# A decode step with its gradients: which small sums share a PSUM bank

## The chip, the cores and the metric

The kernel runs on one core of a Trainium2 chip. The metric is the device time of one execution in microseconds (us). Three runs of the kernel before gave 719.51, 720.91 and 721.76 us, a median of 720.91 us. A separate profiled execution took 720.1 us, of which 718.3 us are the span that the profile covers.

## The reference

One token of width 640 goes through attention over a cache of 8192 keys and values (32 heads of width 128) and, beside it, through a gated layer. The kernel returns the output and the gradients with respect to the token, the caches and the five weight matrices.

```python
def _A_ref(x, k_cache, v_cache, wq, wo):                       # 32 heads, Dh = 128, Sk = 8192
    q = (x @ wq).reshape(B, Sq, Hq, Dh).transpose(0, 2, 1, 3)
    scores = jnp.einsum("bhqd,bhkd->bhqk", q, k) * (Dh ** -0.5)
    p = _softmax(scores, axis=-1)
    o = jnp.einsum("bhqk,bhkd->bhqd", p, v)
    return o.transpose(0, 2, 1, 3).reshape(B, Sq, Hq * Dh) @ wo

def _B_ref(x, w1, w3, w2):                                     # D = 640, F = 1728
    return (_silu(x @ w1) * (x @ w3)) @ w2

xn = _layernorm(x)
out = x + _A_ref(xn, k_cache, v_cache, wq, wo) + _B_ref(xn, w1, w3, w2)
# returned: out, and the gradients of x, k_cache, v_cache, wq, wo, w1, w3, w2 for grad_out
```

For each head the gradients of the two caches are outer products: dV is the probabilities P times the vector do, dK is the score gradients U times the query q. Each is as large as the cache itself, 2 MB a head, so a head reads 4 MB and writes 4 MB.

## The kernel before

A head's 8192 positions lie on 128 partitions with 64 positions (J) each. K and V of a head are tiles of 128 x 64 x 128 in bf16. The kernel first does the gated layer, whose weights are small, and then loops over the heads. The order on every engine is the order of the program text, written out by hand (`manual_schedule`), and the loop is staggered: iteration h finishes head `c` = h, starts head `n` = h + 1 and keeps head `prev` = h − 1's last copy.

One iteration of the loop (lines 717 to 769) runs in this order. The names in capitals of the profile are: PE the TensorE, DVE the VectorE, ACT the ScalarE, POOL the GpSimd engine, SP the queue engine.

- `product(n, "S", 0)`: DVE multiplies half of K by the query into T (L403), PE adds T up with eight matmuls into `psS` (L405).
- `probs(c)`: DVE reads the sum of the exponentials and inverts it (`rZ`, L463), DVE and ACT make P and Pf.
- `outer` (V, half 0): DVE (L425) and ACT (L419, eight instructions) write the outer product into `ot`.
- `keep_dq(prev)`, then a `gap()`, in which one step of a group's preparation or finish may run on ACT and PE.
- `row_dots(c)`: DVE reduces `psDP`, and PE sums the products over the partitions (L503).
- `attend(c)`: sixteen matmuls of V with P into `ob` (L474), and once in a group `on_sums` (L341); `turn_wq(c)`: transposes on PE.
- `product(n, "S", 1)`, `outer` (V, half 1) and its store on POOL's queue (L432), the load of the next V on SP's queue.
- `dscores(c)`: DVE makes U from the sum of L503 (L507), PE adds sixteen matmuls of K with U into `ob`.
- `outer` (K, half 0); ACT copies `ob` out (`wide`, L482) and the turned wq (L522).
- `row_max(n)`: DVE reduces `psS` and takes the row maximum, PE spreads the maxima over the partitions (L450).
- `product(n, "DP", 0)`, and then `blocks_sum(c)`: PE picks o and dq out of `wide` with four f32 matmuls (L490; the profile shows each f32 matmul as two).
- `outer` (K, half 1) and its store, the load of K three heads on, a `gap()`.
- `exps(n)`: DVE reads the spread maxima (`negM`, L455), ACT exponentiates (L458), PE sums over the partitions (L459).
- `product(n, "DP", 1)`.
- `weights(c)`: DVE reads o and dq (`odq`, L527), ACT makes `dq_diag` and `om` from it, PE broadcasts dq (L533), collects o in columns for the group (L538) and adds dq through the turned wq to dxn (L541).

PSUM, the memory that PE writes to, has eight banks of 512 f32 columns on 128 partitions. `accbank` is one bank: columns 0 to 4 hold the running sum dxn (L541), 5 to 9 the running sum out (L341 and L658), 16 to 23 the columns `on_ps` of two groups (written by L538, read by ACT in `on_cols`, L332), 32 to 35 `od` of two heads (written by L490, read by L527). `sm` is another bank, taken anew for each head at L449: column 3 the softmax sum (L459), column 4 the dot sum (L503), columns 8 to 135 the spread maxima (L450). `psS` and `psDP` share two banks, `ob` has one, and three banks (`ps_w`) serve the rest, among them `dx_ps`, in which the dx of the gated layer is summed in parts (`dx_part`).

A matmul's `start` flag says that it opens a sum, `start=False` that it adds to one. dxn and out are never opened by a flag: the bank's first 16 columns are set to zero at L222.

Queues: loads of K and V go out on SP's queue, most stores on POOL's queue. In the profile a store's issue on POOL shows the instruction that the store waited for. `turn_lanes` issues a small load into `lane_pad` on POOL's queue: the kernel counts in `dealt` which of 16 lanes the next transfer of that queue begins at, and the load's number of rows moves that lane on. At iteration H − 3 the stores collected in `late` are issued on POOL, followed by one `turn_lanes(0)`; the stores of the last two heads go out on SP, so nothing follows on POOL.

Of the kernel before, what the change touches and what calls it, by code (L numbers as in the profile page):

```python
# [10 lines left out]
F32 = mybir.dt.float32  # L11
# [5 lines left out]
P = 128  # L17
# [4 lines left out]
def kernel(  # L22
# [80 lines left out]
    with tc.manual_schedule(engines=ORDERED):  # L103
# [29 lines left out]
        def turn_lanes(to):  # L133
            k = (to - dealt[0]) % LANES
            if k:
                rows = k if k > 1 else LANES + 1
                nc.gpsimd.dma_start(lane_pad[0:rows, dealt[1] % 2], wq_v[0:rows, 0:2, 0:8])
                dealt[:] = to % LANES, dealt[1] + 1

        def deal(dst, src, p0, p1):  # L140
            nc.gpsimd.dma_start(dst[p0:p1], src[p0:p1])
            dealt[0] = (dealt[0] + (LANES - 1 if p0 == 0 else P - p0)) % LANES
# [79 lines left out]
        nc.vector.memset(accbank[:, 0:16], 0.0)  # L222
        DXN0 = 0
        OUT0 = NC
        OP0 = 16
        OD0 = 32

        sel = consts.tile([P, P // GH], F32, name="sel")
        nc.vector.tensor_reduce(sel[:], ident_f[:].rearrange("p (q r) -> p q r", r=GH), AX.X, ALU.add)
# [214 lines left out]
        def row_max(st):  # L444
            st.S = small.tile([P, J], F32, name="S_sb", bufs=1)
            nc.vector.tensor_reduce(st.S[:], st.ps["S"][:], AX.X, ALU.add)  # L446
            mrow = small.tile([P, 1], F32, name="mrow")
            nc.vector.tensor_reduce(mrow[:], st.S[:], AX.X, ALU.max)  # L448
            st.sm = ps_s.tile([P, 512], F32, name="sm", tag="sm")  # L449
            nc.tensor.matmul(st.sm[:, 8:8 + P], lhsT=mrow[:].to_broadcast([P, P]), rhs=ident_f[:], start=True, stop=True,  # L450
                             skip_group_check=True)

        def exps(st):
            negM = small.tile([P, 1], F32, name="negM")
            nc.vector.tensor_reduce(negM[:], st.sm[:, 8:8 + P], AX.X, ALU.max, negate=True)  # L455
            st.E = small.tile([P, J], F32, name="E", bufs=1)
            rsum = small.tile([P, 1], F32, name="rsum")
            nc.scalar.activation(st.E[:], st.S[:], ACTF.Exp, bias=negM[:], scale=1.0, accum_out=rsum[:])  # L458
            nc.tensor.matmul(st.sm[:, 3:4], lhsT=ones_f, rhs=rsum[:], start=True, stop=True, skip_group_check=True)  # L459

        def probs(st):
            rZ = small.tile([P, 1], F32, name="rZ")
            nc.vector.reciprocal(rZ[:], st.sm[:, 3:4])  # L463
            st.P2 = small.tile([P, J, 2], BF16, name="P2")
            nc.vector.tensor_scalar(st.P2[:], st.E[:].unsqueeze(2).to_broadcast([P, J, 2]), rZ[:], None, ALU.mult)
            st.Pf = small.tile([P, 2, ACT_J], F32, name="Pf")
            nc.scalar.activation(st.Pf[:], st.E[:].rearrange("p (a j) -> p a j", a=2)[:, :, JH - ACT_J:JH],  # L467
                                 ACTF.Copy, scale=rZ[:])
# [15 lines left out]

        def blocks_sum(st):
            c0 = OD0 + 2 * (st.h % 2)
            st.od = accbank[:, c0:c0 + 2]
            for r in range(WIDE):
                i, b = divmod(r, WIDE // 2)
                nc.tensor.matmul(st.od, lhsT=st.wide[i][:, b * DH:(b + 1) * DH], rhs=pick[:, r, :],  # L490
                                 start=(r == 0), stop=(r == WIDE - 1), skip_group_check=True)
# [6 lines left out]
        def row_dots(st):  # L498
            st.DP = small.tile([P, J], F32, name="DP_sb", bufs=1)
            nc.vector.tensor_reduce(st.DP[:], st.ps["DP"][:], AX.X, ALU.add)  # L500
            rdot = small.tile([P, 1], F32, name="rdot")
            nc.vector.scalar_tensor_tensor(st.S[:], st.DP[:], 1.0, st.P2[:, :, 0], ALU.mult, ALU.mult, accum_out=rdot[:])
            nc.tensor.matmul(st.sm[:, 4:5], lhsT=ones_f, rhs=rdot[:], start=True, stop=True, skip_group_check=True)  # L503

        def dscores(st):
            st.U2 = small.tile([P, J, 2], BF16, name="U2", bufs=1)
            nc.vector.scalar_tensor_tensor(st.U2[:], st.DP[:].unsqueeze(2).to_broadcast([P, J, 2]), st.sm[:, 4:5], st.P2[:],  # L507
                                           ALU.subtract, ALU.mult)
            st.Uf = None
            if st.h < H - 1:  # L510
                st.Uf = small.tile([P, 2, ACT_J], F32, name="Uf")
                nc.vector.tensor_copy(st.Uf[:], st.U2[:, :, 0].rearrange("p (a j) -> p a j", a=2)[:, :, JH - ACT_J:JH])  # L512
            wide_sums(st.K, st.U2, 1)
# [10 lines left out]
        def weights(st):  # L524
            G_, hh = st.G, st.hh
            odq = small.tile([P, 2], F32, name="odq")
            nc.vector.tensor_tensor(odq[:], st.od, sc2[:], ALU.mult)  # L527
            odq_bf = small.tile([P, 1], BF16, name="odq_bf")
            nc.vector.tensor_copy(odq_bf[:], odq[:, 1:2])
            dq_diag = small.tile([P, P], BF16, name="dq_diag", bufs=1)  # L530
            nc.scalar.activation(dq_diag[:], ident_bf[:], ACTF.Copy, scale=odq[:, 1:2])  # L531
            st.ps_db = ps_w.tile([P, DH], F32, name="ps_db", tag="w")
            nc.tensor.matmul(st.ps_db[:], lhsT=ones_bf[:], rhs=dq_diag[:], start=True, stop=True)  # L533
            om = small.tile([P, GH], F32, name="om")
            nc.scalar.activation(om[:], rmask[:], ACTF.Copy, scale=odq[:, 0:1])
            if hh == 0:
                G_["on_ps"] = accbank[:, OP0 + GH * (st.g % 2):OP0 + GH * (st.g % 2 + 1)]
            nc.tensor.matmul(G_["on_ps"][hh * (P // GH):(hh + 1) * (P // GH), :], lhsT=sel[:], rhs=om[:],  # L538
                             start=True, stop=True, skip_group_check=True)
            for ci in range(NC):  # L540
                nc.tensor.matmul(accbank[:, DXN0 + ci:DXN0 + ci + 1], lhsT=st.wqT[:, ci * P:(ci + 1) * P],  # L541
                                 rhs=odq_bf[:], start=False, stop=True, skip_group_check=True)
# [59 lines left out]
        def dx_part(wi, wt, c0, n):  # L602
            T = tpool.tile([P, n, F], BF16, name="T13", tag="T")
            nc.vector.tensor_tensor(T[:], wt[:, c0:c0 + n, :],
                                    bc_sb[:, wi, :].unsqueeze(1).to_broadcast([P, n, F]), ALU.mult)
            for i in range(F // DR1):
                nc.tensor.matmul(dx_ps[:, c0:c0 + n, :], lhsT=ident_bf[:], rhs=T[:, :, DR1 * i:DR1 * (i + 1)],  # L607
                                 start=(wi == 1 and i == 0), stop=(wi == 0 and i == F // DR1 - 1),
                                 skip_group_check=True)

        def grad(wi, wt):
# [82 lines left out]
        def gap():  # L694
            if steps and next(steps[0], "end") == "end":
                steps.pop(0)

        ob = ps_o.tile([P, 512], F32, name="ob", tag="ob")
        nc.tensor.matmul(ob[:], lhsT=ident_bf[:], rhs=zero_bf[:].to_broadcast([P, WIDE * DH]), start=True, stop=True)
        first = new_head(0)  # L700
# [16 lines left out]
        for h in range(H - 1):  # L717
            n = new_head(h + 1) if h + 1 < H else None
            c = hs.pop(h)
            g, hh = divmod(h, GH)  # L720
            if n:
                product(n, "S", 0)
            probs(c)
            outer(c, c.do, c.P2, c.Pf, "V", h, 0)
            if prev:
                keep_dq(prev)
            gap()
            row_dots(c)
            attend(c)
            turn_wq(c)  # L730
            if n:
                product(n, "S", 1)
            outer(c, c.do, c.P2, c.Pf, "V", h, 1)
            if h + 2 < H:
                load_v(h + 2)
            wq_columns(h, 0)
            gap()
            dscores(c)
            outer(c, c.q, c.U2, c.Uf, "K", h, 0)
            keep_rows(c)  # L740
            keep_wq(c)
            if hh == 1 and 0 < g < NG - 1:
                load_wo(g + 1, nc.scalar)
            wq_columns(h, 1)
            if n:
                row_max(n)
                product(n, "DP", 0)
            blocks_sum(c)
            outer(c, c.q, c.U2, c.Uf, "K", h, 1)
            if h == 0:  # L750
                load_k(4)
            elif 1 < h < H - 3:
                load_k(h + 3)
            wq_columns(h, 2)
            if h == H - 3:
                for by, dst, src in late:
                    by(dst, src)
                turn_lanes(0)
            gap()
            if n:  # L760
                exps(n)
                product(n, "DP", 1)
            weights(c)
            gap()
            if hh == 1 and g + 1 < NG:
                steps.append(prep_steps(g + 1))
            if hh == 2:
                gap()
            prev = c
# [88 lines left out]
```

## Time and profile before

| | us |
|---|---|
| median of three runs | 720.91 (719.51 to 721.76) |
| the profiled execution | 720.1 |
| its span | 718.3 |
| DVE busy | 630.6 |
| PE busy (matmuls) | 552.2 |
| ACT busy | 479.3 |
| POOL busy | 49.5 |

The profile gives the time at which each engine was busy with instructions, the granted TensorE clock (1.00 is full speed) and the busy share of the core's 16 DMA engines, all for the whole span or for a chosen stretch. A line of the timeline reads: start in us, duration in us, engine, line of the kernel, operation, what is written from what, with the partitions and elements, and how many instructions were merged; in brackets stands how long the engine was idle before, and what ended the idle time. A line of the waits reads: engine, tile and line that waited, the one waited for, and then us in total, number of times and the longest. The chain of work that ended last gives these shares of the span:

```
DMA 41%; DVE 28%; PE 22%; ACT 5%; issue 1%
```

### The profile page before, as it was taken

To read this page: it belongs to the slowest core of one execution; us is meant where nothing else is said; L and a number is where in the kernel's file an instruction comes from. 1 tells how busy PE (TensorE), PEld (TensorE's weight loads), DVE (VectorE), ACT (ScalarE), POOL (GpSimd) and SP (SyncE) were. 2 spreads that over 40 slices of the span, in tenths; PEclk is the share of its full clock that TensorE was granted. 3 is DMA by queue.
4 is the path that set the end of the run, shared out by engine and by line. 5 is a ranking of instruction groups with operands and counts; after the bars stand their busy time and mean duration, and the time that the engine had idled before them with its cause. 6 is when DMAs were issued, how large, how long until landed. Compare 5 with 4: busy or idle time off the path is not lost.

```text
span 718.3 us, 10242 instructions
## 1 busy us (share of the span) xinstructions
PE 552.2 (77%) x3698; PEld 277.9 (39%) x3698; DVE 630.6 (88%) x722; ACT 479.3 (67%) x1455; POOL 49.5 (7%) x91
## 2 busy tenths in 40 slices
PE   5787788778888797787788787488887878777770
PEld 3653344334444343343343344143443334333330
DVE  5789999899999996798899899499998989999982
ACT  2166666796678856596577866468667957777552
POOL 0010000000000210000000110000000000000100
PEclk9699998997998988799899889889989899999995
DMA  8999999999999999999999999999999999999997
GB/s 354 414 428 425 430 429 430 390 428 428 432 430 429 429 425 426 428 427 429 432 431 428 430 427 424 429 428 427 431 432 428 429 430 430 428 430 431 429 423 309
DMA packets 27696, 303.35 MB, mean 422 GB/s; under 512 B 3264, under 2 KB 3974, under 8 KB 9982
## 3 DMA queue, kind: packets, MB, share of 16 engines
q1 hardware_dynamic: 13490, 154.89, 51.0%
q0 software_dynamic: 10960, 137.72, 45.1%
q10 hardware_dynamic: 3196, 10.10, 3.5%
q8 instruction: 29, 0.48, 0.2%
q14 instruction: 21, 0.17, 0.1%
HBM read 151.34 MB, written 151.34 MB: 421 GB/s over the span
## 4 chain that ended last, share of the span: by engine, by line
DMA 41%; DVE 28%; PE 22%; ACT 5%; issue 1%; SPq 0%; POOL 0%; DVEq 0%; ACTq 0%; POOLq 0%
DMA Kt<-in_A_k_cache_dram 24%; DVE T L403 14%; DMA out_dram<-ot 10%; DVE ot L425 8%; PE ob L474 5%; PE psS L405 5%; PE psDP L405 5%; DMA lane_pad<-in_A_wq_dram 4%; ACT ot L419 3%; DMA Vt<-in_A_v_cache_dram 3%; DMA dbc<-in_B_w_dram 2%; PE accbank L490 1%; DVE DP_sb L500 1%; DVE S_sb L446 1%; PE dx_ps L607 1%
## 5 line engine op out<-in xcount | busy, mean ns | idle before, releaser
L405 PE MATMUL psDP<-T,ident_bf 128*128 128x512 bf16 x512 | 152.2, 451 | 62.1 <-DVE T L403 61.9
L405 PEld LDWEIGHTS <-ident_bf 128*128 128x128 bf16 x1024 | 108.3, 109 | 199.9 <-issue 125.6
L419 ACT ACTIVATE ot<-qs_g,Uf 128x128 bf16<-128x128 bf16 x496 | 151.7, 393 | 41.9 <-DVE Uf L512 26.8
L403 DVE TENSOR_TENSOR T<-Kt,qs_g 128x4096 bf16<-128x4096 bf16 x64 | 146.3, 2286 | 17.4 <-DMA Kt<-in_A_k_cache_dram 16.9
L419 ACT ACTIVATE ot<-do_g,Pf 128x128 bf16<-128x128 bf16 x504 | 153.9, 389 | 1.1
L403 DVE TENSOR_TENSOR T<-Vt,do_g 128x4096 bf16<-128x4096 bf16 x64 | 146.0, 2282 | 2.9 <-ACT do_g L323 1.6
L405 PE MATMUL psS<-T,ident_bf 128*128 128x512 bf16 x512 | 130.2, 400 | 14.9 <-DVE T L403 14.0
L425 DVE TENSOR_TENSOR ot<-qs_g,U 128x3072 bf16<-128x3072 bf16 (+1 forms) x64 | 113.1, 1768 | 13.3 <-DMA out_dram<-ot 13.3
L425 DVE TENSOR_TENSOR ot<-do_g,P 128x3072 bf16<-128x3072 bf16 (+1 forms) x64 | 112.8, 1762 | 6.8 <-DMA out_dram<-ot 5.8
L432 POOL DMA_DIRECT2D out_dram<-ot x60 | 32.2, 537 | 549.9 <-DVE Uf L512 279.3
L474 PE MATMUL ob<-Kt,U 128*4 128x512 bf16 x512 | 60.5, 379 | 1.3 <-DVE U L507 1.3
L474 PE MATMUL ob<-Vt,P 128*4 128x512 bf16 x512 | 61.0, 381 | 0.0
L531 ACT ACTIVATE dq_diag<-ident_bf,odq 128x128 bf16<-128x128 bf16 x32 | 12.8, 401 | 47.2 <-DVE odq L527 47.2
L490 PEld LDWEIGHTS accbank<-pick,wide 128*128 128x128 f32 x256 | 40.1, 223 | 7.8 <-issue 2.4
L467 ACT ACTIVATE Pf<-E,rZ 128x16 f32<-128x16 f32 x32 | 9.8, 305 | 48.4 <-DVE rZ L463 48.4
L297 ACT COPY woT<-ps_t 128x512 bf16<-128x512 bf16 x40 | 23.0, 576 | 21.5 <-PE ps_t L292 21.5
L490 PE MATMUL accbank<-pick,wide 128*128 128x2 f32 x256 | 35.6, 261 | 0.5 <-ACT wide L482 0.5
L450 PE MATMUL sm<-ident_f,mrow 128*128 128x128 f32 x64 | 16.0, 334 | 23.5 <-DVE mrow L448 23.5
L474 PEld LDWEIGHTS <-U 128*4 128x4 bf16 x512 | 19.8, 84 | 36.7 <-DVE U L507 5.2
L474 PEld LDWEIGHTS <-P 128*4 128x4 bf16 x512 | 19.9, 84 | 25.4 <-issue 0.8
L446 DVE TENSOR_REDUCE S_sb<-psS 128x64 f32<-128x512 f32 x32 | 21.9, 685 | 6.0 <-PE psS L405 6.0
L482 ACT COPY wide<-ob 128x256 f32<-128x256 f32 x64 | 19.9, 360 | 8.9 <-PE ob L474 8.9
(165 smaller groups left out, 538.3 us busy)
## 6 DMA issues: line engine op xcount, KB each, us to landing
out_dram<-ot POOLq DMA_DIRECT2D x60, 2048.0 KB, 24.8
Kt<-in_A_k_cache_dram SPq DMA_DIRECT2D x32, 2048.0 KB, 26.4
Vt<-in_A_v_cache_dram SPq DMA_DIRECT2D x32, 2048.0 KB, 21.1
out_dram<-ot SPq DMA_DIRECT2D x8, 1024.0 KB, 13.3
out_dram<-wo_g ACTq DMA_DIRECT2D x6, 640.0 KB, 15.9
wo_g<-in_A_wo_dram ACTq DMA_DIRECT2D x6, 640.0 KB, 15.4
wq<-in_A_wq_dram SPq DMA_DIRECT2D x2, 1280.0 KB, 33.7
w1t<-in_B_w_dram SPq DMA_DIRECT2D x1, 2160.0 KB, 12.3
```

The source lines that it names most:

```text
L297: nc.scalar.copy(woT[:], ps_t[:])
L403: nc.vector.tensor_tensor(T[:], src[:, :, ds_], vec[:, ds_].unsqueeze(1).to_broadcast([P, J, DHH]), ALU.mult)
L405: nc.tensor.matmul(ps[:], lhsT=ident_bf[:], rhs=T[:, :, RUN * i:RUN * (i + 1)], start=(half == 0 and i == 0), stop=(half == 1 and i == DHH ...
L419: nc.scalar.activation(st.ot[half][:, JH - ACT_J + j].rearrange("p a b -> p (a b)"), vec, ACTF.Copy, scale=wf[:, half, j:j + 1])
L425: nc.vector.tensor_tensor(st.ot[half][:, 0:n], vec.rearrange("p (a b) -> p a b", b=2).unsqueeze(1).to_broadcast([P, n, DH // 2, 2]), w2[:, ...
L432: nc.gpsimd.dma_start(dst.rearrange("p j d -> p (j d)"), st.rows[:])
L446: nc.vector.tensor_reduce(st.S[:], st.ps["S"][:], AX.X, ALU.add)
L450: nc.tensor.matmul(st.sm[:, 8:8 + P], lhsT=mrow[:].to_broadcast([P, P]), rhs=ident_f[:], start=True, stop=True, skip_group_check=True)
L474: nc.tensor.matmul(ob[c0:c0 + WIDE, :], lhsT=w2[:, WIDE * q:WIDE * (q + 1), 0], rhs=src[:, WIDE * q:WIDE * (q + 1), :].rearrange("p j d -> ...
L482: nc.scalar.copy(part[:], ob[:, i * (WIDE // 2) * DH:(i + 1) * (WIDE // 2) * DH])
L490: nc.tensor.matmul(st.od, lhsT=st.wide[i][:, b * DH:(b + 1) * DH], rhs=pick[:, r, :], start=(r == 0), stop=(r == WIDE - 1), skip_group_che ...
L531: nc.scalar.activation(dq_diag[:], ident_bf[:], ACTF.Copy, scale=odq[:, 1:2])
```

## The change

Four edits.

1. `sm` is taken once, ahead of the loop, and not once for each head. The softmax sum moves to column 0, the dot sum to column 1; the maxima stay at columns 8 to 135.
2. `od` (o and dq of a head, four columns) and `on_ps` (eight columns) move out of `accbank` into `sm`, to columns 136 to 139 and 140 to 147. `accbank` holds only dxn and out after that.
3. In `dx_part` the flag that opens a sum is set only at the first matmul of the first part (c0 = 0), where it was set at the first matmul of each of the three parts.
4. `mark_lanes` is new: eight loads on POOL's queue, of two rows and 3, 5, 6, 7, 9, 10, 11 and 12 bf16 elements, into rows of `lane_pad` from partition 32 on. It is called once, behind `turn_lanes(0)` at iteration H − 3.

```diff
+        def mark_lanes():
+            for i, n in enumerate((3, 5, 6, 7, 9, 10, 11, 12)):
+                r = STRIP + 2 * i
+                nc.gpsimd.dma_start(lane_pad[r:r + 2].rearrange("p a b c -> p (a b c)")[:, 0:n], wq_v[0:2, 0, 0:n])
...
-        OP0 = 16
-        OD0 = 32
+        Z0 = 0
+        DOT0 = 1
+        MAX0 = 8
+        OD0 = MAX0 + P
+        OP0 = OD0 + 4
...
-            st.sm = ps_s.tile([P, 512], F32, name="sm", tag="sm")
-            nc.tensor.matmul(st.sm[:, 8:8 + P], lhsT=mrow[:].to_broadcast([P, P]), rhs=ident_f[:], start=True, stop=True,
+            nc.tensor.matmul(sm[:, MAX0:MAX0 + P], lhsT=mrow[:].to_broadcast([P, P]), rhs=ident_f[:], start=True, stop=True,
                              skip_group_check=True)
...
-            nc.vector.tensor_reduce(negM[:], st.sm[:, 8:8 + P], AX.X, ALU.max, negate=True)
+            nc.vector.tensor_reduce(negM[:], sm[:, MAX0:MAX0 + P], AX.X, ALU.max, negate=True)
...
-            nc.tensor.matmul(st.sm[:, 3:4], lhsT=ones_f, rhs=rsum[:], start=True, stop=True, skip_group_check=True)
+            nc.tensor.matmul(sm[:, Z0:Z0 + 1], lhsT=ones_f, rhs=rsum[:], start=True, stop=True, skip_group_check=True)
...
-            nc.vector.reciprocal(rZ[:], st.sm[:, 3:4])
+            nc.vector.reciprocal(rZ[:], sm[:, Z0:Z0 + 1])
...
-            st.od = accbank[:, c0:c0 + 2]
+            st.od = sm[:, c0:c0 + 2]
...
-            nc.tensor.matmul(st.sm[:, 4:5], lhsT=ones_f, rhs=rdot[:], start=True, stop=True, skip_group_check=True)
+            nc.tensor.matmul(sm[:, DOT0:DOT0 + 1], lhsT=ones_f, rhs=rdot[:], start=True, stop=True, skip_group_check=True)
...
-                G_["on_ps"] = accbank[:, OP0 + GH * (st.g % 2):OP0 + GH * (st.g % 2 + 1)]
+                G_["on_ps"] = sm[:, OP0 + GH * (st.g % 2):OP0 + GH * (st.g % 2 + 1)]
...
-                                 start=(wi == 1 and i == 0), stop=(wi == 0 and i == F // DR1 - 1),
+                                 start=(wi == 1 and c0 == 0 and i == 0), stop=(wi == 0 and i == F // DR1 - 1),
...
+        sm = ps_s.tile([P, 512], F32, name="sm", tag="sm")
         ob = ps_o.tile([P, 512], F32, name="ob", tag="ob")
...
                 turn_lanes(0)
+                mark_lanes()
```

More of the change, by code (lines that the diff above doesn't have):

```diff
@@ L502, in row_dots @@
             nc.vector.scalar_tensor_tensor(st.S[:], st.DP[:], 1.0, st.P2[:, :, 0], ALU.mult, ALU.mult, accum_out=rdot[:])
-            nc.tensor.matmul(st.sm[:, 4:5], lhsT=ones_f, rhs=rdot[:], start=True, stop=True, skip_group_check=True)
+            nc.tensor.matmul(sm[:, DOT0:DOT0 + 1], lhsT=ones_f, rhs=rdot[:], start=True, stop=True, skip_group_check=True)
         def dscores(st):
             st.U2 = small.tile([P, J, 2], BF16, name="U2", bufs=1)
-            nc.vector.scalar_tensor_tensor(st.U2[:], st.DP[:].unsqueeze(2).to_broadcast([P, J, 2]), st.sm[:, 4:5], st.P2[:],
+            nc.vector.scalar_tensor_tensor(st.U2[:], st.DP[:].unsqueeze(2).to_broadcast([P, J, 2]), sm[:, DOT0:DOT0 + 1], st.P2[:],
                                            ALU.subtract, ALU.mult)
```

## The prediction

> **What bounds the kernel now.** First the page: the span, the busy shares and the DMA row of the forty slices.
>
> ```profile
> span 718.3 us, 10242 instructions
> PE 552.2 (77%) x3698; PEld 277.9 (39%) x3698; DVE 630.6 (88%) x722; ACT 479.3 (67%) x1455; POOL 49.5 (7%) x91
> ...
> DMA  8999999999999999999999999999999999999997
> ```
>
> The DMA engines are full from the second slice to the last but one; the rates are 414 to 432 GB/s but for one slice of 390. The 303.35 MB at 430 GB/s are 705 us, so the DMA is the first bound. VectorE (DVE) is the second: I read the period of a head as the distance between two reads `negM` (L455). The first is at 55.8 us, the last at 687.1, so 31 heads take 631.3 us, 20.36 us each; heads in which DVE never idles take 18.71 or 18.72. The third view is what DVE waited for from 56 to 690 us (total us, times, longest):
>
> ```profile
> DVE ot L425 <- DMA out_dram<-ot: 19.1, 4, 10.1
> DVE T L403 <- DMA Kt<-in_A_k_cache_dram: 16.9, 12, 4.1
> ...
> DVE odq L527 <- PE accbank L490: 4.0, 9, 1.1
> ...
> DVE T L403 <- DMA Vt<-in_A_v_cache_dram: 1.1, 2, 0.9
> ```
>
> 19.1 + 16.9 + 1.1 = 37.1 us of DVE's time is waiting for DMA. That is all the cover the DMA gives to new waits on DVE: 37.1 / 31 = 1.20 us a head. The fourth view is the timeline, here of the head at 503 us (start, duration, engine and line):
>
> ```profile
> 503.15 0.49 PE L450 MATMUL sm<-ident_f,mrow 128*128 128x128 f32 x2 [0.73 <-DVE mrow L448]
> ...
> 505.21 1.75 DVE L425 TENSOR_TENSOR ot<-qs_g,U 128x3072 bf16<-128x3072 bf16 x1
> 505.35 3.35 PE L405 MATMUL psDP<-T,ident_bf 128*128 128x512 bf16 x8 [1.71 <-DVE T L403]
> ...
> 506.88 0.28 DVE L455 TENSOR_REDUCE negM<-sm 128x1 f32<-128x128 f32 x1
> ...
> 507.08 2.28 DVE L403 TENSOR_TENSOR T<-Vt,do_g 128x4096 bf16<-128x4096 bf16 x1
> ...
> 508.54 0.95 PE L490 MATMUL accbank<-pick,wide 128*128 128x2 f32 x8
> ...
> 509.35 0.36 PE L459 MATMUL sm<-rsum,ones_fc 128*128 128x1 f32 x2
> ...
> 509.52 0.16 DVE L527 TENSOR_TENSOR odq<-accbank,sc 128x2 f32<-128x2 f32 x1 [0.17 <-PE accbank L490]
> 509.57 1.89 PE L405 MATMUL psDP<-T,ident_bf 128*128 128x512 bf16 x8
> ...
> 511.44 0.23 PE L538 MATMUL accbank<-om,sel 128*32 128x4 f32 x2
> ...
> 511.99 0.16 DVE L463 RECIPROCAL rZ<-sm 128x1 f32<-128x1 f32 x1
> ```
>
> The reader should see the order on TensorE (PE): the maximum (L450), eight sums psDP, then blocks_sum (L490). DVE reads the maximum at 506.88, while those eight sums still run and blocks_sum has not begun. That is possible because L450 writes `sm` and L490 writes `accbank`.
>
> **Does a read wait for its columns or for its bank?** One place of the trace can tell: the last `on`, which reads accbank columns 20 to 23. L538 writes these; L541, behind it, writes columns 0 to 4.
>
> ```profile
> 700.22 0.22 PE L538 MATMUL accbank<-om,sel 128*32 128x4 f32 x2
> 700.28 0.27 ACT L548 CAST dqbc_g<-ps_db 128x128 bf16<-128x128 f32 x1
> 700.38 0.28 PE L541 MATMUL accbank<-odq_bf,wqT 128*128 128x1 bf16 x5
> 700.69 0.16 ACT L332 COPY on<-accbank 128x4 f32<-128x4 f32 x1
> ```
>
> Its columns were done at 700.44 and ScalarE (ACT) was free at 700.55, yet it starts at 700.69, 0.03 us after L541 ends at 700.66. Elsewhere an unblocked ACT instruction starts up to 0.1 us before the one ahead ends (141.91 behind 141.77 + 0.24). So I take it that accesses are ordered by bank. It is one row, and the other reading is a rival below.
>
> The Trainium skill ("PSUM — Partial Sum Buffer", section "PSUM bank collisions raise a hardware error") asks for PSUM to be guarded by bank and quadrant, not by address, and says that a compiler orders any two accesses of different engines to one bank. By it the time is the forecast; by columns it would be that of the unchanged rival. The row agrees with the page.
>
> **The change, part by part.**
>
> *A new wait of negM for blocks_sum.* The two now share `sm`, and L490 stands ahead of negM in program order (lines 748 and 761). Its price without any other shift is the end of the L490 group less the start of negM, head by head: 508.54 + 0.95 − 506.88 = 2.61 us here. Read so over the 31 heads, 18 give 1.14 or 1.15, one 0.58, and 12 give 2.26 to 3.54 (mean 2.76). Sum: 18 × 1.14 + 0.58 + 33.1 = 54.2 us. What parts them is the clock: the eight sums take 1.89 us in a 1.14 head and 3.35 here. The granted clock was 0.67 from 503.6 to 508.7, and 1.00 from 436.4 to 440.8, a 1.14 head. Behind negM on DVE queue T of the second psDP half, odq, and T of the next head; Exp on ACT and then L459 and eight psDP sums on PE wait for these.
>
> *rZ now waits for L538*, which moves into its bank. Here L538 ends at 511.67 and rZ starts at 511.99, so it looks free. But its cover goes: psDP at 509.57 no longer starts with T long done, but with T's end. From psDP's start to L538's end is 2.10 us at full clock, from the end of the T ahead of odq (507.08 + 2.28) to rZ is 2.63, so still no wait there. At half clock psDP takes 3.35 to 3.57, 1.5 to 1.7 more, and rZ waits 1.0 to 1.2. I take 1.2 in 12 heads: 14.4 us. Bounds: 0, and 31 × 1.2 = 37.
>
> *odq now waits for L459.* From negM's end (507.16), Exp (0.35, accumulator read 0.19) and L459 (0.36) need about 0.95 us; T between negM and odq takes 2.28 and covers it. Without that cover the late case is a busy ACT: at 268.8 us a wo_g step ahead of Exp makes L459 end 3.2 us after odq. I take 2 us in all; bounds 0 and the 7.4 that all heads give as they stand.
>
> *Taken off.* odq's 4.0 us for L490 are inside the new wait. `on` no longer waits for L541: 0.24 us at the end, and no idle is booked before the seven others. L503 may wait for `on` once a group; U, its reader, comes 3.4 us later (496.66 to 500.02), so nothing. The single `sm` tile removes no wait that the page books.
>
> *One start flag fewer in dx* leaves the same 18 matmuls a part: 0, since a flag is no instruction.
>
> *Eight tiny loads.* POOL's last issue in the trace is lane_pad at 670.40, 0.95 us long; eight more at the 0.60 to 0.98 of these rows are 5 to 8 us on an engine with nothing behind, under stores that run to 718. None reads or writes what another waits for. If each had to wait for a late store (these land 35 to 39 us after issue, so about 709), the last would still be issued before the end. I take 0, bounds 0 and 5.
>
> **The sum.** DVE's end of work is 705.3. Less the DMA waits, plus the new ones: 705.3 − 37.1 + 54.2 + 14.4 + 2 − 4.0 = 734.8. DMA need is then 705 us of some 750, still 94%, so waits in clumps stay; between 0 and 37.1 I take a quarter, 9.3: 744.1. Behind that the span has 13.0 us of stores now, which is backlog (1 MB half stores land in 13.3); with the backlog gone I take the 4.9 us of the quickest transfer of that size (w2t, 960 KB): 749.0. The profiled run was 720.1 for a span of 718.3, the median of the runs 720.91: 1.8 outside the span. That gives 750.8; I say **750 us**, 4% slower.
>
> **The rivals.**
>
> *Hidden behind the DMA (not slower).* If PE keeps its full clock, the new wait is 1.14 × 31 = 35.3 us, less than the 37.1 of cover. It decides at 1.20 us a head. Then 705.3 − 37.1 + 35.3 + 2 − 4.0 = 701.5 for the work, and the DMA still sets the end: 718 to 725 with clumps. For it: 18 heads of 31 give 1.14. Against: 12 do not, and the cover is not where the waits are (four store waits hold 19.1 us of it).
>
> *Slow clock everywhere.* The wait opens gaps on PE in every head: about 0.9 us until L459, then 1.3 until T ends. If each head then runs at half clock: 31 × (2.76 + 1.2) + 2 − 4.0 = 120.8, so 705.3 − 37.1 + 120.8 + 4.9 + 1.8 = 796. For it: the slow psDP rows follow idle time of 1.7 to 2 us. Against: equally long gaps stand before fast ones.
>
> The Trainium skill ("TensorE: Matmul & The Clock Gate", section "What's actually happening") gives the array full clock only behind a busy window of some 3.4 us and takes it away after an idle one. By that rule more gaps mean more slow heads, which is this rival; the rows show both clocks behind like gaps, so they bear it out in part.
>
> *Columns, not banks.* If 0.24 us at one row misleads, no wait is added: odq's and `on`'s are unchanged or gone, and the time is 718 to 722. The change would do what it says and cost nothing.
>
> **How the numbers follow.** Forecast 0.58, hidden 0.18, slow clock 0.14, columns 0.10. Faster or slower counts beyond 0.3%, 2.2 us, which is what runs of 719.51 to 721.76 can tell. Columns gives 0.03 faster and 0.07 same; hidden 0.02, 0.05 and 0.11 slower; the other two are slower. So 0.05, 0.12, 0.83. The range reaches from 722, where most of the hidden case lies, to 790, short of the slow case's end; the forecast's own range is 735 (no DMA waits left, some of rZ's hidden) to 775.
>
> **What would show it.** negM booked as waiting for PE L490, 1.1 to 3 us in nearly every head, 45 to 85 us in all; DVE's waits for DMA down from 37.1 to near 10; the period at 21 us or more; the DMA row below full; the stores behind DVE's last work down from 13 to about 5 us. The forecast is wrong if negM starts straight behind `ot` as now, or if it waits and the DMA's share stays at 1.00.

## The result and the profile after

The changed kernel takes 770.64 us (median of 4 runs, 770.23 to 773.88), beside 720.21 us (719.36 to 721.76) for the kernel before. The ratio is 1.0707, with a 95% interval of 1.0672 to 1.0743: 50 us slower, where 750 us in a range of 722 to 790 had been forecast. The profiled run has a span of 768.8 us. Where the runs of a kernel spread, its ratio is taken over those within 1.5% of its fastest.

The page of the changed kernel, the same rows as before:

```profile
span 768.8 us, 10250 instructions
PE 585.1 (76%) x3698; PEld 286.1 (37%) x3698; DVE 634.2 (82%) x722; ACT 479.1 (62%) x1455; POOL 53.6 (7%) x99
...
DMA  8999989999989999999989999999989999899946
```

DVE's work has hardly grown (630.6 to 634.2 us), and the bytes are the same. But the DMA row now has dips, and its rate over the span fell from 421 to 394 GB/s: the DMA no longer sets the pace. What DVE waited for, from 56 to 740 us:

```profile
DVE negM L462 <- PE sm L497: 56.4, 31, 2.8
DVE rZ L470 <- PE sm L545: 33.6, 29, 1.5
DVE T L411 <- ACT do_g L331: 4.3, 7, 0.6
```

(Line numbers moved: L462 is negM, once L455; L497 blocks_sum, once L490; L545 the columns on_ps, once L538; L470 rZ, once L463; L413 the sums psDP and psS, once L405; L466 the softmax sum, once L459. In later runs the numbers move on by a few.) No wait for DMA is left in this stretch; there were 37.1 us. In their place stand two waits for matmuls that write other columns of the bank that is read. One head from the timeline:

```profile
534.30 3.42 PE L413 MATMUL psDP<-T,ident_bf 128*128 128x512 bf16 x8 [1.71 <-DVE T L411]
...
537.55 0.95 PE L497 MATMUL sm<-pick,wide 128*128 128x2 f32 x8
538.54 0.29 DVE L462 TENSOR_REDUCE negM<-sm 128x1 f32<-128x128 f32 x1 [2.63 <-PE sm L497]
...
539.36 0.38 PE L466 MATMUL sm<-rsum,ones_fc 128*128 128x1 f32 x2 [0.86 <-ACT E L465]
540.95 0.15 DVE L534 TENSOR_TENSOR odq<-sm,sc 128x2 f32<-128x2 f32 x1
541.09 3.44 PE L413 MATMUL psDP<-T,ident_bf 128*128 128x512 bf16 x8 [1.34 <-DVE T L411]
...
544.51 0.23 PE L545 MATMUL sm<-om,sel 128*32 128x4 f32 x2
...
544.77 0.17 DVE L470 RECIPROCAL rZ<-sm 128x1 f32<-128x1 f32 x1 [1.28 <-PE sm L545]
```

negM starts 0.04 us behind the end of blocks_sum, after 2.63 us of waiting. PE, which had worked through without a pause here, now waits 0.86 us for Exp and 1.34 us for T. Its next eight sums then run at half clock: 3.44 us, with a granted clock of 0.53 from 541.0 to 544.5, where it had been 1.00 from 537.5 to 540.8. L545 ends that much later, and rZ waits another 1.28 us. The period of a head is (738.83 − 55.92) / 31 = 22.03 us, against 20.36.

### The profile page after: what moved, and what is told of

Read it like the earlier page. It is cut to its first block, busy times and chain, and to the rows that moved or that the text cites. A ratio compares the mean times of both kernels' runs of the same rounds, so it can differ in the third digit from the quotient of the medians.

```text
span 768.8 us, 10250 instructions
## 1 busy us (share of the span) xinstructions
PE 585.1 (76%) x3698; PEld 286.1 (37%) x3698; DVE 634.2 (82%) x722; ACT 479.1 (62%) x1455; POOL 53.6 (7%) x99
## 3 DMA queue, kind: packets, MB, share of 16 engines
q0 software_dynamic: 11216, 137.73, 42.3%
## 4 chain that ended last, share of the span: by engine, by line
DVE 55%; PE 36%; ACT 4%; issue 2%; DMA 2%; SPq 0%; DVEq 0%; ACTq 0%
DVE T L411 26%; PE psDP L413 23%; DVE ot L433 16%; PE sm L497 4%; ACT ot L427 2%; DVE S_sb L454 2%; DVE DP_sb L507 2%; PE ob L481 2%; PE psS L413 2%; DMA dbc<-in_B_w_dram 2%; ACT do_g L331 1%; DVE negM L462 1%; DVE P L472 1%; DVE U L514 1%; PE ps_d L323 1%
## 5 line engine op out<-in xcount | busy, mean ns | idle before, releaser
L413 PE MATMUL psDP<-T,ident_bf 128*128 128x512 bf16 x512 | 180.6, 517 | 92.6 <-DVE T L411 92.6
L413 PEld LDWEIGHTS <-ident_bf 128*128 128x128 bf16 x1024 | 114.2, 115 | 233.6 <-issue 172.9
L413 PE MATMUL psS<-T,ident_bf 128*128 128x512 bf16 x512 | 131.7, 404 | 1.2 <-DVE T L411 1.2
L462 DVE TENSOR_REDUCE negM<-sm 128x1 f32<-128x128 f32 x32 | 9.3, 291 | 56.4 <-PE sm L497 56.4
L538 ACT ACTIVATE dq_diag<-ident_bf,odq 128x128 bf16<-128x128 bf16 x32 | 12.9, 402 | 57.1 <-DVE odq L534 57.1
L465 ACT ACTIVATE E<-S_sb,negM 128x64 f32<-128x64 f32 x32 | 11.1, 347 | 53.2 <-DVE negM L462 53.2
L497 PEld LDWEIGHTS sm<-pick,wide 128*128 128x128 f32 x256 | 41.0, 228 | 8.2 <-issue 3.8
L497 PE MATMUL sm<-pick,wide 128*128 128x2 f32 x256 | 36.2, 263 | 0.5 <-ACT wide L489 0.5
L470 DVE RECIPROCAL rZ<-sm 128x1 f32<-128x1 f32 x32 | 5.4, 168 | 37.3 <-PE sm L545 37.3
L466 PE MATMUL sm<-rsum,ones_fc 128*128 128x1 f32 x64 | 13.7, 282 | 24.3 <-ACT E L465 24.3
```

What stands on the lines that cost most here:

```text
L413: nc.tensor.matmul(ps[:], lhsT=ident_bf[:], rhs=T[:, :, RUN * i:RUN * (i + 1)], start=(half == 0 and i == 0), stop=(half == 1 and i == DHH ...
L462: nc.vector.tensor_reduce(negM[:], sm[:, MAX0:MAX0 + P], AX.X, ALU.max, negate=True)
L466: nc.tensor.matmul(sm[:, Z0:Z0 + 1], lhsT=ones_f, rhs=rsum[:], start=True, stop=True, skip_group_check=True)
```

## The experiments

Every kernel ran beside the kernel before on the same chip; the ratios are to that one, with 95% intervals. The edits stand against the changed kernel.

**Both back in accbank.**

```diff
-            st.od = sm[:, c0:c0 + 2]
+            st.od = accbank[:, c0:c0 + 2]            # c0 = 32 + ..., as before
-                G_["on_ps"] = sm[:, OP0 + GH * (st.g % 2):OP0 + GH * (st.g % 2 + 1)]
+                G_["on_ps"] = accbank[:, 16 + GH * (st.g % 2):16 + GH * (st.g % 2 + 1)]
```

> od and on_ps go back into accbank; the single sm tile, the one start flag and the eight loads stay. As in the kernel before, matmuls with a start flag share the bank of dxn and out. Theory (reads wait for the bank): the waits of negM (56.4 us) and rZ (37.3 us) go, DVE again waits for DMA, 718 to 723 us. Rival (the single tile, the flag or the eight loads cost time): the time stays well above, up to 770.

721.88 us, ratio 1.0025 (1.0013 to 1.0038). No wait of negM or rZ is booked, and DVE waits for DMA again (17.0 + 16.5 + 3.4 us from 56 to 705). All but 0.25% of the loss lies in the place of these two slices.

**One of the two back.** The first line of that diff alone, then the second alone.

> Only od goes back into accbank, on_ps stays in sm. (As in the kernel before, matmuls with a start flag share the bank of dxn and out.) Theory: negM waits 0; with T ahead of time again, psDP's second half starts earlier and rZ waits for L545 at most in heads with a slow clock, some 15 us, hidden behind the DMA: 719 to 726 us. Rival (the two waits are independent): rZ keeps 37 us, which is all the cover there is: 724 to 740 us.

724.38 us, ratio 1.0055 (1.0038 to 1.0072). Waits of DVE from 56 to 705 us:

```profile
DVE rZ L470 <- PE sm L545: 22.3, 15, 3.7
DVE ot L433 <- DMA out_dram<-ot: 13.1, 4, 8.6
DVE T L411 <- DMA Kt<-in_A_k_cache_dram: 9.8, 9, 1.7
```

rZ waits in 15 heads and not in 29, so its wait depends in large part on the first one. Of its 22.3 us, 14.2 came out of the waits for DMA, which fell from 37.1 to 22.9 us, and the kernel lost 0.55%.

> Only on_ps goes back into accbank, od stays in sm. (As in the kernel before, matmuls with a start flag share the bank of dxn and out.) Theory: negM keeps its 56 us, rZ waits 0, so 770.6 - 37.3 = 733 plus what DMA waits come back: 732 to 742 us. Rival (PE's late second half of psDP moves the wait to the next reader, DP_sb): DVE waits there instead and the time stays above 755.

747.27 us (median of four), ratio 1.034 (1.028 to 1.0401); the runs spread from 740.34 to 751.47. The profiled run is the lowest, with these waits from 56 to 705 us:

```profile
DVE negM L462 <- PE sm L497: 43.8, 30, 3.5
DVE S_sb L454 <- PE psS L413: 8.0, 7, 1.5
DVE T L411 <- DMA Kt<-in_A_k_cache_dram: 6.3, 3, 3.8
DVE T L411 <- DMA Vt<-in_A_v_cache_dram: 4.7, 2, 3.3
```

rZ does not wait any more, although the second half of psDP took more than 2.2 us in 29 of 31 heads. The time is a few us above what was expected: in the profiled run DVE waits 8.0 us at S_sb, after 4.1 in the same stretch before, and 11.7 for DMA. The rival had looked for the wait at DP_sb, another reader. Why the runs of this kernel spread by 11 us, and those of the kernel before by 2.5, was not tried.

**blocks_sum behind exps.** The layout of the change, another order.

```diff
-            blocks_sum(c)
             outer(c, c.q, c.U2, c.Uf, "K", h, 1)
...
                 exps(n)
-                product(n, "DP", 1)
+            blocks_sum(c)
+            if n:
+                product(n, "DP", 1)
             weights(c)
```

> The layout of the change, but blocks_sum is issued behind exps(n), so on PE behind L466, and negM has no write to the bank between it and the maximum. Theory (negM's wait comes from the order in the shared bank): negM waits 0, odq waits a little for blocks_sum, psDP's second half is not late, 719 to 735 us. Rival (sharing the bank costs whatever the order): above 750.

734.06 us, ratio 1.0185 (1.014 to 1.0231), from 729.55 to 737.53; the profiled run is the highest. In it negM waits for nothing. odq now waits 26.4 us for blocks_sum, which on PE stands behind L466 and so behind Exp, and rZ still waits 19.7 us: psDP's second half took more than 2.2 us in 21 heads, which the theory had not expected. The sharing of the bank costs by the order, as the theory had it, but this order is not a free one.

**Idle PE time filled.**

```diff
-        nc.vector.memset(accbank[:, 0:16], 0.0)
+        nc.vector.memset(accbank[:], 0.0)
...
+        def fill(n):
+            for _ in range(n):
+                nc.tensor.matmul(accbank[:, 128:512], lhsT=ident_bf[:], rhs=g_bc_bf[:, 0:384],
+                                 start=False, stop=True, skip_group_check=True)
...
             blocks_sum(c)
+            fill(4)
...
                 exps(n)
+                fill(5)
```

> The changed kernel with idle PE time filled: four matmuls of 384 columns behind blocks_sum and five behind L466, into columns 128 to 511 of accbank that nobody reads (the outputs are unchanged). Theory (rZ waits because psDP's second half runs at half clock behind the gap): that half takes 1.9 us and not 3.6, rZ's 37.3 us fall below 10, negM's 56 stay: 733 to 745 us. Rival (rZ's wait comes from the order alone, the clock is a side effect): rZ stays above 25 us, 760 us or more.

Four runs lie between 734.51 and 748.01 us, median 743.08. The ratio 1.0225 (1.0195 to 1.0255) rests on the two lower ones, 734.51 and 738.67; the profiled run is one of the upper two, with a span of 745.5 us. Why they spread was not tried. In the profiled run DVE's waits from 56 to 705 us are:

```profile
DVE negM L462 <- PE sm L502: 48.2, 30, 3.5
...
DVE rZ L470 <- PE sm L550: 0.3, 1, 0.3
```

With nine useless matmuls a head rZ waits 2.3 us over the whole span instead of 37.3 (1.9 of them in the last head), and the kernel is 23 to 36 us faster than the changed one's median. The order in the bank is the same as in the changed kernel, but the second half of psDP now takes 1.89 us in 31 of 32 heads and 2.04 in one. So the slow clock decides whether rZ has to wait here. It needs the order too: in on_back the second half took as long as in the changed kernel in most heads, but L545 wrote another bank, and rZ did not wait.

> As fill_half1, with eight more such matmuls ahead of psDP's first half. Theory (what is left of negM's wait above 1.14 us a head is half clock): negM waits 35 to 40 us in all, about the cover of 37 us that the DMA gives, and DVE waits for DMA again: 722 to 735 us. Rival (the wait is a fixed price of the order): negM stays above 50 us and the time as in fill_half1.

With `fill(8)` ahead of psDP's first half as well: 726.27 us, ratio 1.008 (1.0062 to 1.0099).

```profile
DVE negM L462 <- PE sm L502: 36.5, 31, 3.5
DVE ot L433 <- DMA out_dram<-ot: 9.4, 2, 6.9
DVE T L411 <- DMA Kt<-in_A_k_cache_dram: 3.3, 1, 3.3
```

Of the 31 waits of negM 30 take 1.09 to 1.20 us, close to the 1.14 of a head at full clock, and one 3.5. DVE waits for DMA again. That is the rival "hidden behind the DMA" of the prediction, with its condition brought about by hand; the time is just above the 718 to 725 that it named.

**Both moved.** The change's layout, with blocks_sum between Exp and L466, and L545 one iteration later.

```diff
-        def exps(st):
+        def exps(st, c=None):
...
             nc.scalar.activation(st.E[:], st.S[:], ACTF.Exp, bias=negM[:], scale=1.0, accum_out=rsum[:])
+            if c:
+                blocks_sum(c)
             nc.tensor.matmul(sm[:, Z0:Z0 + 1], lhsT=ones_f, rhs=rsum[:], start=True, stop=True, skip_group_check=True)
...
-            nc.tensor.matmul(G_["on_ps"][hh * (P // GH):(hh + 1) * (P // GH), :], lhsT=sel[:], rhs=om[:],
-                             start=True, stop=True, skip_group_check=True)
+            st.om = om
...
             if prev:
+                on_sum(prev)                         # the matmul taken out above
                 keep_dq(prev)
...
-            blocks_sum(c)
             outer(c, c.q, c.U2, c.Uf, "K", h, 1)
...
-                exps(n)
+                exps(n, c)
```

> The layout of the change (od and on_ps in sm, dxn and out alone), two moves in PE's order: blocks_sum between Exp and L466, and the matmul of on_ps (L545) one iteration later, ahead of keep_dq. Theory (only the place of these two writes between a write and its read costs): negM and rZ wait about 0 each, odq little, DVE waits for DMA as before: 718 to 725 us. Rival (a shared bank costs in any order): 730 us or more, with waits at odq or rZ.

722.37 us, ratio 1.0029 (1.0017 to 1.0042). negM and rZ wait for nothing; odq waits 11.6 us for L466 (L468 in this run) and 1.2 for blocks_sum, under the DMA, for which DVE waits 38.3 us.

**The last quarter of a per cent.** The three runs are both_back without the eight loads and with the old flags; both_back without the loads; both_moved without the loads.

> both_back (which was 0.25% above before) without the eight loads and with the old start flags; of the change only the single sm tile and its column numbers are left. (As in the kernel before, matmuls with a start flag share the bank of dxn and out.) Theory (both_back's 0.25% came from the loads or the flag): ratio 0.998 to 1.001. Rival (it comes from the single tile, or is spread between builds): 1.001 to 1.004.

719.76 us, ratio 0.9995 (0.9983 to 1.0007).

> both_back without the eight loads, the one start flag kept, so that loads and flag are told apart. (As in the kernel before, matmuls with a start flag share the bank of dxn and out.) Theory (the chain of both_back ends with a late store's landing, then a load that waited for it: the loads set the end and cost some 2 us): as one_tile, ratio 0.998 to 1.001. Rival (the flag makes the difference): 1.001 to 1.004 as in both_back.

720.40 us, ratio 1.0 (0.999 to 1.001). The flag makes no difference; the loads do. In both_back the chain of waits ends so (start, us):

```profile
669.25 38.89 DMA out_dram<-wq
708.14 0.28 issue
708.42 0.50 POOL lane_pad L143
```

A late store lands 38.89 us after its issue, and one of the eight loads had waited for it; the last two are issued up to 709.46. They land after 7.3 us, at 715.69 and 716.20, which is still ahead of the last store (dwq_t, 717.52). What ends late is POOL's drain, an instruction at the end of the program that here ended 3.4 to 3.7 us behind the landing of the last load on POOL's queue, in back_no_loads (708.68 to 712.09) as in the changed kernel (738.13 to 741.86). Here are the drains of POOL and SP in both_back, and then in back_no_loads (shortest, median and longest in ns, and when the first and the last of the three start):

```profile
L864 POOLq DRAIN  x3: 46/102/10998, 708.9 to 720.4; - x3
L864 SPq DRAIN  x3: 7/7/13, 717.9 to 720.2; - x3
```

```profile
L863 POOLq DRAIN  x3: 46/102/40212, 671.9 to 717.8; - x3
L863 SPq DRAIN  x3: 7/7/13, 717.2 to 717.6; - x3
```

POOL's long drain in both_back runs from 708.93 to 719.93, 3.7 us beyond the landing of its last load and 2.0 us beyond SP's second drain (717.93). In back_no_loads it ends at 712.1, 5.2 us ahead of SP's. So the loads cost some 2 us by way of POOL's drain; the span is 720.7 us. In od_back POOL's drain ends at 716.29 and SP's at 721.24, so the 0.55% there is not owed to the loads by its trace.

> both_moved without the eight loads: the banks and the start flag of the change with the order that needs no wait. Theory: the 0.29% of both_moved goes as well, ratio 0.998 to 1.001, no version below the DMA's bound. Rival (odq's 12 us in the shared bank cost something): 1.001 to 1.004.

720.80 us, ratio 1.0006 (0.9998 to 1.0015): the banks and the flag of the change at no measurable cost. In both_moved POOL's drain ends only 0.2 us behind SP's, so its trace shows little of the 0.29% that the loads cost there. No version came out below the kernel before by more than the noise.

## Why the prediction was right, and where it was off

**A read waits for the bank.** Right. Of the two readings of `on`'s 0.24 us, the one by bank holds: negM is booked 31 times behind L497, which does not write its columns. In both_moved no such write stands between, and the wait is gone with the layout unchanged. So the rival "columns, not banks" falls. Two things stay open. Each of these banks is one tile of the kernel, so these runs cannot tell a wait by bank from a wait by tile. And the profile infers these waits from semaphores, which the program sets; what the chip would do without them, no run shows.

**The price of negM's wait.** 54.2 us forecast from the rows of before, 56.4 measured: 17 heads wait 1.09 or 1.10 us and 14 wait 2.48 to 2.83, where the rows had 12 slow heads. One of those rows, 0.58, was read short; its whole group gives 1.14, and the rows then give 54.8.

**The price of rZ's wait: the term that was mis-sized.** 14.4 us forecast, 37.3 measured over the whole span (30 times), just at the upper bound of 37 that had been named. I took 1.2 us in 12 heads, the share of slow heads that the first half of psDP showed before. The size of one wait was right, 1.16 us on average in 29 heads; the last head waits 3.7, with no next head's work to cover it. The share was not: the new gaps stand ahead of the second half, and that half took more than 2.2 us in 30 of 31 heads, while the first half was slow in 14. The prediction had seen those gaps, 0.9 and 1.3 us, and used them only for the rival "slow clock everywhere"; that rival came true for one of the two halves. fill_half1 shows that the gaps are the cause of the slow half, and on_back that the slow half delays rZ only through the shared bank.

The Trainium skill ("TensorE: Matmul & The Clock Gate", section "What's actually happening") lowers the clock after an idle window of some 3.4 us. The rows show half clock after 0.86 and 1.34 us of idle time with 0.38 us of work between; an idle stretch of 3.4 us was not needed here.

**odq and `on`.** odq cost nothing against L466, for which 2 us had been taken: the T between covered it. `on` against L510 was priced at nothing; PE did wait for it there, 4.3 us in six groups, and DVE did not wait for PE in turn.

**What DMA waits remain.** 9.3 us were left in the sum; 0 came. With the period at 22 us the DMA had enough spare time for its clumps to vanish.

**The sum again.** DVE's work ends at 760.4, forecast 744.1. The difference of 16.3 us is rZ (+22.9), negM (+2.2), odq (−2), DMA waits (−9.3) and some 2.5 us of others: DVE's busy time grew by 3.6, its waits for do_g by 2.7 and T's wait for psDP came to 1.2, while S_sb's waits fell from 6.0 to 2.0 and rZ's old wait of 0.7 is gone. Behind DVE's work come 8.4 us and not 4.9: I had taken a load, and the last transfers are stores, of which `dwq_t` lands in 8.3 us. Together: span 749.0 forecast, 768.8 measured. So 30 us of loss were forecast and 50 came. The range of 722 to 790 holds the result because it reached towards the case of a slow clock in every head. The forecast's own 735 to 775 holds it with little to spare, and by luck: rZ's term was 22.9 us too low, and had the 9.3 us of DMA waits come as forecast, the time would have been near 780 by this sum.

**The eight loads.** 0 forecast, within 0 and 5. In the changed kernel the last is issued at 733.0 us, long before the end, so 0 holds by its trace. Where the rest of the time is won back they can set the end: both_back against back_no_loads is 0.25% of 720, 1.8 us. The prediction held it enough that the last load is issued before the end, under stores that run to 718. It left out that the load needs a landing of its own, 7.2 us in both_back, and that POOL's drain ends another 3.7 us later.

**Flag and single tile.** 0, as forecast: one_tile and back_no_loads.

## What to carry to other kernels

Count small results that share a PSUM bank as one resource. As the waits of this program go, a write from PE between another result's write and its read delays that read, whatever the columns, so put such writes behind the read; two moves of a line made this layout free. When a wait opens a gap ahead of a run of matmuls, price the run at half clock as well, and check what waits for its end. An engine's slack under a DMA bound (here 1.20 us a head) is a budget: a wait of 22 us cost 0.55% here, and the two waits of 94 us together cost 7%.

## What was not expected of the hardware

Useless work made a kernel faster: nine and then seventeen matmuls of 384 columns a head, which keep the granted clock up (0.939 and 0.967 over the span, 0.854 in the changed kernel), took 3 to 5% and nearly 6% off.

A load of 12 to 48 bytes is no small thing to a full queue: the eight took 12 to 39 us to land for the first five in both_back and 7 to 9 for the last three, and the packets of one queue rose by 256 (10960 to 11216 on q0), 32 for each load of two rows.
